# Fused soft-cap attention and soft mixture of experts: the tail products of a pair's first four tiles moved forward, constant products between the first transposes, and two more tiles of exponentials on VectorE

## The chip, the cores and the metric

The kernel runs on one core of one Trainium2 chip. The metric is the device time of one execution in microseconds (us), the median of several runs. Engines are called by the profiler's short names: PE is TensorE (PEld its weight loads), ACT is ScalarE, DVE is VectorE, POOL is GpSimd, SP is SyncE, which here only issues transfers.

## The reference

For each of 8 batches and 12 heads, with 448 tokens of 64 values, attention with a soft cap is computed; its output is the input x of a soft mixture of experts with 32 slots and 8 experts:

```
scores = cap * tanh(scale * q @ k.T / cap)          with cap = 30, scale = 1/8
attn = exp(scores - max), divided by its sum over the keys
x = attn @ v                                        3584 tokens of 768
logits = x @ phi                                    768 -> 32 slots
d = softmax of logits over all tokens;  c = softmax over the slots
slot_input = d.T @ x
slot_out[e] = relu(slot_input[e] @ w1[e]) @ w2[e]   4 slots for each expert e
out = c @ slot_out
```

(The lines say in short what the reference's Python computes.)

## The kernel before

**Tiles and pairs.** The 448 tokens of a head lie as 64 partitions with 7 tokens each. Two heads share the 128 partitions and are called a pair; there are 48 pairs, four heads (two pairs) make a quad Q, and three quads a batch. A pair has 7 key tiles c; one tile is 128 partitions (two heads of 64 keys) by 448 queries. All 336 tiles stand in one order (`turn`), in which the two pairs of a quad alternate, and are cut into 56 chunks j of 6 tiles. Seven chunks are one batch, the period in which the work repeats.

**A chunk.** PE computes the scores of three tiles at a time into one of two score buffers in PSUM (`qk_chunk`, L292). ACT takes the tanh of three tiles (`tanh_chunk`, L301) into a tile `ex` in SBUF; there are five such tiles (NEX), used in rotation, so that chunk j can only be written when the products that read chunk j-5 are done. ACT then takes the exponential of a whole chunk in place (`exp_chunk`, L305). In some chunks, the list `shared`, the first of the six tiles is left out of this and its exponential is computed by DVE in five steps, a polynomial (`poly_exp`, L327, L329 to L332): steps 0 and 1 in the slot a of the chunk's own iteration, 2 and 3 in its slot d, step 4 in the slot a of the next one. The exponential of a shared chunk covers 5 x 448 = 2,240 columns on ACT, of another 2,688.

**The product with v.** When all 7 tiles of a pair are there, PE multiplies them with v (`pv_mms`, L350). Queries are taken in three groups of 128 (128 x 128 weights) and a last group of 64, the tail, which takes two products of 64 x 64 a tile. A column of ones beside v gives the sum of the exponentials. The products of one pair gather in one PSUM bank (pool psV, one buffer). `pv_first` does the three large groups of tiles 0 to 3 (CA = 4), 12 products; `pv_rest` does those of tiles 4 to 6, 9 products, then the tails of tiles 0 to 3 (8 products) and of 4 to 6 (6 products), and ends with `norm`: DVE takes a reciprocal (L357) and multiplies the bank into xq (L358), which frees the bank for the next pair.

**The order of work.** It is written by hand. One iteration of the main loop emits the tanh of chunk j, the exponential of chunk j-1, then, if a pair is due, `pv_first`, slot a, the first scores for chunk j+1, slot b, `pv_rest`, slot c, the second scores, slot d. Everything else hangs in these slots: filling products on PE without use for the result (`fill`, L378, into unused columns of the pair's bank, and `spare` through `busy`, L589), the transposes of x (`x_transp`, L393 and L398, copied by DVE in L404), the transposes of the next quads' k and q (`transp`, L260, copied by DVE in L262), the cast of v on POOL (`vcast`, L270 and L271), logits, slot sums, and the loads of weights, which POOL issues. The transposes share one PSUM bank (pool psT). Each engine goes through its own instructions in the order in which they were emitted.

**The start.** Before the loop the first pair's q and k come in by small loads; 29 constant products run on PE (L589, `busy`), then `first_half(0)` casts, transposes and copies the first pair in pieces listed by hand (`first_pieces`, L215, L219, L221).

**After the loop** follow the last two pairs, the experts (from about 269 us) and the output.

Of the kernel before, what the change touches and what calls it, by code (L numbers as in the profile page):

```python
# [19 lines left out]
NT = 7  # L20
# [3 lines left out]
CS = 3  # L24
NG = 4
NF = 3
# [10 lines left out]
def kernel(  # L37
# [20 lines left out]
    cap = float(cap)  # L58
# [6 lines left out]
    NCH = NTILE // CH  # L65
# [3 lines left out]
    pe, dve, act, pool, sp = nc.tensor, nc.vector, nc.scalar, nc.gpsimd, nc.sync  # L69
# [109 lines left out]
    def load(nm, Q):  # L179
        if Q < NQ:  # L180
            t = raw_tile(nm)
            (sp if nm == "v" else pool).dma_start(out=t, in_=quad_ap(nm, Q))  # L182
            raws[nm, Q] = t
# [25 lines left out]
    def first_pieces(h, jobs):  # L209

        for stage, nm, c0, c1, eng, bank, at0 in jobs:
            copy = act.copy if eng is act else dve.tensor_copy
            cols = slice(h * HP, h * HP + HP)
            if stage == "cast":
                copy(casts[nm, 0][:, c0:c1, cols],  # L215
                     raws[nm, 0][h][:, c0 * DH:c1 * DH].rearrange("p (c d) -> p c d", d=DH))
            elif stage == "turn":
                for c in range(c0, c1):
                    pe.transpose(bank[cols, at0 + c - c0, :], casts[nm, 0][:, c, cols], ident)  # L219
            else:  # L220
                copy(qkT[nm, 0][cols, c0:c1, :], bank[cols, at0:at0 + c1 - c0, :])  # L221

    def first_half(h):
        for nm in ("k", "q"):
            if h == 0:
                qkT[nm, 0] = qk.tile([P, NT, P], BF16, name=nm + "T", tag=nm + "T")
        one = psT.tile([P, 8, P], BF16, name="ps1", tag="T")
        two = psV.tile([P, NT, P], BF16, name="ps2", tag="pv")
        if h == 0:

            first_pieces(h, (("cast", "k", 0, CS, dve, None, 0), ("cast", "q", 0, 4, dve, None, 0),
                             ("cast", "q", 4, NT, act, None, 0), ("turn", "k", 0, CS, pe, two, 0),
                             ("copy", "k", 0, CS, dve, two, 0), ("turn", "q", 0, 4, pe, one, 0),
                             ("cast", "k", CS, NT, act, None, 0),
                             ("copy", "q", 0, 4, dve, one, 0), ("turn", "q", 4, NT, pe, two, CS),
                             ("copy", "q", 4, NT, act, two, CS), ("turn", "k", CS, NT, pe, one, 4),
                             ("copy", "k", CS, NT, dve, one, 4)))
        else:
            first_pieces(h, (("cast", "k", 0, NT, dve, None, 0), ("cast", "q", 0, NT, dve, None, 0),
                             ("turn", "k", 0, NT, pe, two, 0), ("turn", "q", 0, NT, pe, one, 0),  # L240
                             ("copy", "k", 0, NT, dve, two, 0), ("copy", "q", 0, NT, dve, one, 0)))
            for nm in ("q", "k"):
                raws.pop((nm, 0)), casts.pop((nm, 0))
                load(nm, 2)
# [36 lines left out]
    scores, exs, pvs, xq, xTs, lgs = {}, {}, {}, {}, {}, {}  # L281
# [13 lines left out]
    def tanh_chunk(i):  # L295
        j, half = divmod(i, CH // CS)
        if half == 0:
            exs[j] = exps[j % NEX].tile([P, CH, S], BF16, name="ex", tag="ex")
        sc = scores.pop(i)
        for u0, u1 in ((0, 1), (1, CS)) if i == 0 else ((0, CS),):  # L300
            act.activation(exs[j][:, half * CS + u0:half * CS + u1, :],  # L301
                           sc[:, u0:u1, 0:S], ACT.Tanh, scale=qk_scale / cap)
# [4 lines left out]
    def exp_chunk(j):  # L307
        exp_part(j, 1 if j in shared else 0, CH)
# [3 lines left out]
    PARTS = {0: ((0, "a", (0, 1)), (0, "d", (2, 3)), (1, "a", (4,))),  # L312
             1: ((0, "a", (0, 1)), (0, "d", (2, 3)), (1, "a", (4,))),
             2: ((0, "a", (0, 1)), (0, "d", (2, 3)), (1, "a", (4,))),
             3: ((0, "a", (0, 1)), (0, "d", (2, 3)), (1, "a", (4,))),
             6: ((0, "a", (0, 1)), (0, "d", (2, 3)), (1, "a", (4,)))}
    shared = [j for j in range(NCH - 2) if j % 7 in PARTS and j > 7] if cap < 50 else []

    lead = POW2[0] / FRAC ** 3
    p2, p1, p0 = (c / POW2[0] * FRAC ** (n + 1) for n, c in enumerate(POW2[1:]))  # L320
# [15 lines left out]
    def pv_mms(pr, c0, c1, gs, dst):  # L336

        Q, h = divmod(pr, 2)
        for tail in (False, True):
            for c in range(c0, c1):  # L340
                j, u = divmod(place[pr, c], CH)
                for g in gs:
                    if (g == NF) != tail:
                        continue
                    for n in range(2 if tail else 1):
                        r = slice(n * HP, n * HP + HP) if tail else slice(0, P)
                        q0, s0 = g * P, 2 * (g - gs[0])
                        out_, v_ = (dst[r, s0, :], vbds[Q % 2][r, h, c, n * W:n * W + W]) \
                            if tail else (dst[:, s0:s0 + 2, :], vbds[Q % 2][:, h, c, :])
                        pe.matmul(out_, exs[j][r, u, q0:q0 + (HP if tail else P)], v_,  # L350
                                  start=(c == 0 and g == gs[0]), stop=(c == NT - 1),
                                  skip_group_check=True)

    def norm(pr, s0, s1, pv):
        Q, h = divmod(pr, 2)
        rec = xs.tile([P, NT, 1], F32, name="rec", tag="rec", bufs=4)[:, 0:s1 - s0, :]
        dve.reciprocal(rec, pv[:, 0:s1 - s0, DH:W])  # L357
        dve.tensor_tensor(xq[Q][:, h, s0:s1, :], pv[:, 0:s1 - s0, 0:DH],  # L358
                          rec.to_broadcast([P, s1 - s0, DH]), op=ALU.mult)
# [6 lines left out]
    CA, homes = 4, {}  # L366

    def pv_first(pr):
        xq_tile(pr)
        homes[pr] = psV.tile([P, 512], F32, name="pv", tag="pv")  # L370
        pvs[pr] = homes[pr][:, 0:NT * W].rearrange("p (t w) -> p t w", w=W)
        pv_mms(pr, 0, CA, (0, 1, 2), pvs[pr])

    def fill(n):

        home = homes[max(homes)][:, NT * W:]
        for _ in range(n):
            pe.matmul(home, ones, ones[:, 0:512 - NT * W], start=False, stop=True,  # L378
                      skip_group_check=True)

    def pv_rest(pr):
        pv_mms(pr, CA, NT, (0, 1, 2), pvs[pr])
        for c0, c1 in ((0, CA), (CA, NT)):
            pv_mms(pr, c0, c1, (NF,), pvs[pr][:, 2 * NF:NT, :])
        norm(pr, 0, NT, pvs.pop(pr))

    def turn_x(ps, q0, pr, gs):
# [12 lines left out]
    def x_transp(pr):  # L400
        ps = psT.tile([P, S], BF16, name="xps", tag="T")
        turn_x(ps, 0, pr, range(NG))
        t = xs.tile([P, S], BF16, name="xT", tag="xT", bufs=2)
        dve.tensor_copy(t, ps)  # L404
        xTs[pr] = t
# [38 lines left out]
    def e_norm(b):  # L444

        ps = psT.tile([P, 1], F32, name="zps", tag="T")
        for g in range(NG):
            r = slice(0, P if g < NF else HP)
            pe.matmul(ps, e4s[b][r, g, :], ones[r, 0:1], start=(g == 0), stop=(g == NG - 1))
        if b == 0:  # L450
            dve.tensor_copy(zacc, ps)
        else:
            dve.tensor_tensor(zacc, ps, zacc, op=ALU.add)
        if b == B - 1:
            dve.reciprocal(rz, zacc)
# [76 lines left out]
    for b in range(B):  # L532
        j = b * PER
# [44 lines left out]
    def run(j, slot):  # L578
        for f, a in aux.pop((j, slot), []):
            f(*a)  # L580
# [6 lines left out]
    def busy(n, home=None):  # L587
        for _ in range(n):
            pe.matmul(junk if home is None else home, ones, ones, start=True, stop=True)  # L589

    busy(4)
    junk = boots[1][:, 0, 0:P]
    busy(25)
    first_half(0)
    qk_chunk(0)
    qk_chunk(1)
# [6 lines left out]
    for j in range(NCH):  # L603
        run(j, "0")
        tanh_chunk(2 * j)
        if j == NCH - 1:
            exp_chunk(j - 1)
        tanh_chunk(2 * j + 1)
        run(j, "e")
        if j < 2:  # L610
            exp_chunk(j)
        elif 2 < j < NCH - 1:
            exp_chunk(j - 1)
        pr = pair_at.get(j - 2)
        if pr is not None:
            pv_first(pr)
        run(j, "a")
        if j == NCH - 1:
            pv_rest(pr)
            busy(8, psT.tile([P, P], F32, name="filler", tag="T"))  # L620
            e_norm(B - 2)
            x_transp(pr)

            id32 = xs.tile([P, P], F32, name="id32", tag="lg", bufs=2)
            pool.tensor_copy(id32, ident)
            break
        qk_chunk(2 * j + 2)
        run(j, "b")
        if pr is not None:
            pv_rest(pr)  # L630
        run(j, "c")
        qk_chunk(2 * j + 3)
        run(j, "d")
# [186 lines left out]
    for n in range(B // 2 * NT):  # L820
        bb, c = divmod(n, NT)
# [11 lines left out]
        for half in range(2):  # L833
            pe.matmul(op[:, half, 0:HD], et_tile(bb, c), so[half],
                      start=True, stop=True)
# [47 lines left out]
```

## Time and profile before

| | |
|---|---|
| median of 11 runs | 313.56 us (312.86 to 315.72) |
| profiled execution: its own time | 313.02 us |
| its span, from the first to the last instruction | 311.3 us |
| mean granted clock of TensorE | 0.984 |
| PE, ACT, DVE, POOL busy | 267.0, 272.7, 208.4, 134.0 us |
| HBM read, written | 91.32, 18.87 MB |

The profile is of one execution. Busy times are sums over the whole span and overlap between engines. Waits name the engine and line that ended an engine's idle time. The chain that ended last is followed back from the last instruction: at each step to what released it, or to the instruction before it on its engine. Starts of matrix products are recorded; their ends are modelled, so that a stretch of products is best measured from start to start.

### The profile page before, as it was taken

To read this page: it belongs to the slowest core of one execution; us is meant where nothing else is said; L and a number is where in the kernel's file an instruction comes from. 1 tells how busy PE (TensorE), PEld (TensorE's weight loads), DVE (VectorE), ACT (ScalarE), POOL (GpSimd) and SP (SyncE) were. 2 spreads that over 40 slices of the span, in tenths; PEclk is the share of its full clock that TensorE was granted. 3 is DMA by queue.
4 is the path that set the end of the run, shared out by engine and by line. 5 is a ranking of instruction groups with operands and counts; after the bars stand their busy time and mean duration, and the time that the engine had idled before them with its cause. 6 is when DMAs were issued, how large, how long until landed. Compare 5 with 4: busy or idle time off the path is not lost.

```text
span 311.3 us, 11337 instructions
## 1 busy us (share of the span) xinstructions
PE 267.0 (86%) x5063; PEld 189.4 (61%) x5063; DVE 208.4 (67%) x453; ACT 272.7 (88%) x209; POOL 134.0 (43%) x176
## 2 busy tenths in 40 slices
PE   8898888889998989998999899888999899998820
PEld 6675666666666666666666667666766678642400
DVE  3613358759975998499848995899478944236840
ACT  4999999999999999999999999999999997136730
POOL 4574373466447545653473448244912250000000
PEclk9999999999999999999999999999999999999985
DMA  7999999799999999999799999999999549938997
GB/s 238 234 203 202 204 177 192 146 225 200 207 187 219 211 194 188 221 196 212 132 201 202 211 189 205 205 201 204 193 203 202 143 133 324 336 150 314 392 412 298
DMA packets 57489, 67.75 MB, mean 218 GB/s; under 512 B 3809, under 2 KB 53601, under 8 KB 57441
## 3 DMA queue, kind: packets, MB, share of 16 engines
q0 software_dynamic: 42448, 35.31, 73.7%
q1 hardware_dynamic: 14704, 31.50, 29.8%
q8 instruction: 39, 0.64, 0.8%
q10 hardware_dynamic: 288, 0.23, 0.2%
q14 instruction: 10, 0.07, 0.1%
HBM read 91.32 MB, written 18.87 MB: 354 GB/s over the span
## 4 chain that ended last, share of the span: by engine, by line
PE 39%; DVE 38%; ACT 15%; issue 2%; DMA 1%; DVEq 0%; ACTq 0%
PE pv L350 10%; ACT ex L301 7%; DVE xq L358 6%; ACT ex L305 6%; DVE work L330 5%; DVE ex L332 4%; DVE work L331 4%; PE sc L292 4%; PE junk L589 4%; DVE work L329 3%; DVE xT L404 3%; DVE work L327 3%; PE kps L260 2%; DVE qT L262 2%; DVE kT L262 2%; PE so_ps L754 2%
## 5 line engine op out<-in xcount | busy, mean ns | idle before, releaser
L301 ACT ACTIVATE ex<-sc 128x1344 bf16<-128x1344 f32 (+1 forms) x113 | 143.6, 1376 | 3.5 <-PE pv L350 2.4
L305 ACT ACTIVATE ex<-ex 128x2240 bf16<-128x2240 bf16 (+4 forms) x58 | 130.8, 2259 | 0.1
L350 PE MATMUL pv<-vbd,ex 128*128 128x130 bf16 (+1 forms) x1610 | 86.4, 210 | 13.7 <-DVE xq L358 10.5
L350 PEld LDWEIGHTS <-ex 128*128 128x128 bf16 (+1 forms) x1680 | 72.4, 101 | 33.5 <-DVE xq L358 9.9
L292 PE MATMUL sc<-qT,kT 64*64 64x448 bf16 x672 | 69.6, 359 | 3.9 <-ACT ex L301 2.2
L270 POOL CAST vbd<-vraw 64x896 bf16<-64x896 f32 x23 | 21.4, 929 | 84.8 <-PE pv L350 81.0
L404 DVE COPY xT<-xps 128x448 bf16<-128x448 bf16 x47 | 18.3, 389 | 25.6 <-PE xps L398 24.9
L441 POOL COPY e<-E 128x512 bf16<-128x512 bf16 x9 | 5.5, 616 | 65.8 <-ACT E L435 31.7
L358 DVE TENSOR_TENSOR xq<-pv,rec 128x448 bf16<-128x448 f32 x46 | 28.7, 624 | 1.6
L330 DVE SCALAR_TENSOR_TENSOR work<-work 128x448 f32<-128x448 uint16 x33 | 26.9, 817 | 0.0
L292 PEld LDWEIGHTS <-kT 64*64 64x64 bf16 x672 | 21.7, 105 | 8.5 <-issue 5.6
L110 POOL DMA_DIRECT2D w1b<-in_moe_w_dram x32 | 24.7, 775 | 0.0
L589 PEld LDWEIGHTS <-ones 128*128 128x128 bf16 x320 | 19.5, 102 | 7.5 <-issue 4.3
L378 PE MATMUL pv<-ones 128*128 128x57 bf16 x620 | 23.9, 188 | 0.0
L271 POOL CAST vbd<-vraw 64x896 bf16<-64x896 f32 x23 | 22.4, 976 | 1.4
L589 PE MATMUL junk<-ones 128*128 128x128 bf16 x283 | 20.6, 220 | 1.7 <-DVE xq L358 1.3
L331 DVE SCALAR_TENSOR_TENSOR work<-work 128x448 f32<-128x448 f32 x33 | 21.3, 644 | 1.1
L262 DVE COPY kT<-kps 128x896 bf16<-128x896 bf16 x23 | 14.3, 622 | 11.4 <-PE kps L260 10.8
L332 DVE SCALAR_TENSOR_TENSOR ex<-work 128x448 bf16<-128x448 f32 x33 | 21.0, 636 | 0.2
L378 PEld LDWEIGHTS <-ones 128*128 128x128 bf16 x620 | 20.7, 96 | 0.3
L262 DVE COPY qT<-qps 128x896 bf16<-128x896 bf16 x23 | 14.3, 622 | 8.3 <-PE qps L260 8.3
L182 POOL DMA_DIRECT2D qb<-in_q_dram x22 | 16.4, 744 | 3.4 <-DVE casts L215 3.4
(117 smaller groups left out, 337.6 us busy)
## 6 DMA issues: line engine op xcount, KB each, us to landing
w1b<-in_moe_w_dram POOLq DMA_DIRECT2D x32, 384.0 KB, 8.7
vraw<-in_v_dram SPq DMA_DIRECT2D x23, 448.0 KB, 5.0
w2d<-in_moe_w_dram POOLq DMA_DIRECT2D x20, 384.0 KB, 9.2
w2t<-w2d SPq DMA_DIRECT2D x20, 384.0 KB, 5.1
out_dram<-ob SPq DMA_DIRECT2D x8, 768.0 KB, 7.1
qb<-in_q_dram POOLq DMA_DIRECT2D x22, 224.0 KB, 8.3
kb<-in_k_dram POOLq DMA_DIRECT2D x22, 224.0 KB, 7.1
w2b<-in_moe_w_dram POOLq DMA_DIRECT2D x12, 384.0 KB, 8.5
```

The source lines that it names most:

```text
L262: dve.tensor_copy(t, ps)
L292: pe.matmul(sc[cs, u, 0:S], qkT["k", Q][r, c, cs], qkT["q", Q][r, :, cs], start=True, stop=True)
L301: act.activation(exs[j][:, half * CS + u0:half * CS + u1, :], sc[:, u0:u1, 0:S], ACT.Tanh, scale=qk_scale / cap)
L305: act.activation(exs[j][:, u0:u1, :], exs[j][:, u0:u1, :], ACT.Exp, scale=cap)
L330: lambda: dve.scalar_tensor_tensor(xp, frac, p2, frac, ALU.add, ALU.mult),
L331: lambda: dve.scalar_tensor_tensor(xp, xp, p1, frac, ALU.add, ALU.mult),
L332: lambda: dve.scalar_tensor_tensor(t, xp, p0, xb, ALU.add, ALU.mult))
L350: pe.matmul(out_, exs[j][r, u, q0:q0 + (HP if tail else P)], v_, start=(c == 0 and g == gs[0]), stop=(c == NT - 1), skip_group_check=True)
L358: dve.tensor_tensor(xq[Q][:, h, s0:s1, :], pv[:, 0:s1 - s0, 0:DH], rec.to_broadcast([P, s1 - s0, DH]), op=ALU.mult)
L378: pe.matmul(home, ones, ones[:, 0:512 - NT * W], start=False, stop=True, skip_group_check=True)
L404: dve.tensor_copy(t, ps)
L589: pe.matmul(junk if home is None else home, ones, ones, start=True, stop=True)
```

## The change

Three edits are made together.

The 8 tail products of tiles 0 to 3 leave `pv_rest` and become a call of their own, `pv_tail(pr, 0, CA)`, after slot a of the pair's iteration and before the first scores for chunk j+1. For this, the flag `start`, which makes a bank begin anew, is given by the first large product of a pair alone and no longer by its first tail.

In the start's list, the word `fill` stands three times; each puts two constant products (`busy(2)`, 128 x 128 each) on PE: behind the transposes of the first four q tiles, behind those of the last q tiles, and behind those of the last k tiles.

In the list of shared chunks, j > 7 becomes j > 5, so that chunks 6 and 7 are shared too: 35 chunks in place of 33.

```diff
@@ first_pieces
-            if stage == "cast":
+            if stage == "fill":
+                busy(c0)
+            elif stage == "cast":
@@ first_half
-                             ("cast", "k", CS, NT, act, None, 0),
+                             ("cast", "k", CS, NT, act, None, 0), ("fill", "", 2, 0, pe, None, 0),
                              ("copy", "q", 0, 4, dve, one, 0), ("turn", "q", 4, NT, pe, two, CS),
-                             ("copy", "q", 4, NT, act, two, CS), ("turn", "k", CS, NT, pe, one, 4),
-                             ("copy", "k", CS, NT, dve, one, 4)))
+                             ("copy", "q", 4, NT, act, two, CS), ("fill", "", 2, 0, pe, None, 0),
+                             ("turn", "k", CS, NT, pe, one, 4), ("copy", "k", CS, NT, dve, one, 4),
+                             ("fill", "", 2, 0, pe, None, 0)))
@@ shared chunks
-    shared = [j for j in range(NCH - 2) if j % 7 in PARTS and j > 7] if cap < 50 else []
+    shared = [j for j in range(NCH - 2) if j % 7 in PARTS and j > 5] if cap < 50 else []
@@ pv_mms
-                                  start=(c == 0 and g == gs[0]), stop=(c == NT - 1),
+                                  start=(c == 0 and g == gs[0] < NF), stop=(c == NT - 1),
@@ pv_rest
+    def pv_tail(pr, c0, c1):
+        pv_mms(pr, c0, c1, (NF,), pvs[pr][:, 2 * NF:NT, :])
+
     def pv_rest(pr):
         pv_mms(pr, CA, NT, (0, 1, 2), pvs[pr])
-        for c0, c1 in ((0, CA), (CA, NT)):
-            pv_mms(pr, c0, c1, (NF,), pvs[pr][:, 2 * NF:NT, :])
+        pv_tail(pr, CA, NT)
         norm(pr, 0, NT, pvs.pop(pr))
@@ main loop
         if pr is not None:
             pv_first(pr)
         run(j, "a")
+        if pr is not None:
+            pv_tail(pr, 0, CA)
```

## The prediction

> **What bounds the kernel now.** I read the page first: PE 86%, ACT 88%, DVE 67% busy. Two engines at nearly the same share say that an average cannot name the bound, so I went on to the waits. From the page and then from the view of waits:
>
> ```profile
> PE 267.0 (86%) x5063; PEld 189.4 (61%) x5063; DVE 208.4 (67%) x453; ACT 272.7 (88%) x209; POOL 134.0 (43%) x176
> ...
> DVE rec L357 <- PE pv L350: 10.1, 20, 2.3
> ...
> ACT ex L301 <- PE pv L350: 2.4, 5, 0.8
> ...
> PE sc L292 <- ACT ex L301: 2.2, 3, 1.0
> ```
>
> ACT waits five times for PE to release a tile of exponentials (five buffers, NEX), and it does so only late. PE waits for ACT only three times, all before 49 us. The timeline of ACT tells when the late waits come:
>
> ```profile
> 142.67 2.22 ACT L305 ACTIVATE ex<-ex 128x2240 bf16<-128x2240 bf16 x1
> 145.32 2.47 ACT L301 ACTIVATE ex<-sc 128x1344 bf16<-128x1344 f32 x2 [0.43 <-PE pv L350]
> ```
>
> An exp of 2,240 columns holds ACT for 1.96 us where nothing waits (starts 49.17 and 51.13), so here 145.32 - 142.67 - 1.96 = 0.69 us are lost. Over the run such losses add up to about 4.3 us. Without them a period of seven chunks takes ACT 31.04 us (exp starts 57.97 and 89.01). But the start-to-start distance of the same xq product in the chain is 31.51, 31.68, 31.98, 31.93, 31.96 and 32.24 us (50.62, 82.13, 113.81, 145.79, 177.72, 209.68, 241.92): something slower than ACT sets it. The chain that ended last, from 141 to 179 us, has no ACT piece:
>
> ```profile
> 150.34 0.64 DVE xq L358
> ...
> 151.02 0.86 PE pv L350 x12
> ...
> 152.31 0.17 PE xps L398 x2
> ...
> 152.50 0.40 DVE xT L404
> 152.90 0.04 issue
> 152.95 0.58 PE kps L260 x14
> 153.53 0.89 PE pv L350 x19
> ...
> 157.11 0.40 DVE xT L404
> 157.51 0.04 issue
> 157.56 0.58 PE qps L260 x14
> 158.14 0.90 PE pv L350 x19
> ```
>
> So from 49 to 266 us the bound is PE and DVE in turns: ACT to about 48 us, then this relay, whose idle ACT only mirrors. The reader is to see the two places a period where PE's kps or qps waits for DVE's copy xT (they share the one psT bank). The timeline of PE shows what that wait costs:
>
> ```profile
> 148.07 0.56 PE L292 MATMUL sc<-qT,kT 64*64 64x448 bf16 x6
> 148.57 0.96 PE L350 MATMUL pv<-vbd,ex 128*128 128x130 bf16 x19
> ...
> 151.02 0.86 PE L350 MATMUL pv<-vbd,ex 128*128 128x130 bf16 x12 [0.63 <-DVE xq L358]
> 151.72 0.43 PE L378 MATMUL pv<-ones 128*128 128x57 bf16 x10
> ...
> 152.25 0.59 PE L292 MATMUL sc<-qT,kT 64*64 64x448 bf16 x6
> 152.95 0.58 PE L260 MATMUL kps<-ident,kb 128*64 128x128 bf16 x14
> ```
>
> Six score products hold PE 0.50 us when nothing follows late (148.07 to 148.57) and 0.70 us here: 0.20 us of idle PE.
>
> **Tails moved ahead of the first score chunk.** Eight products and their weight loads move; no DMA, copy or queue goes with them. Price of one: pv_first's twelve large products take 151.72 - 151.02 = 0.70 us, 0.058 each. In pv_rest, 9 large and 14 tails run from 153.46 to the next scores at 154.23, 0.77 us; less 9 x 0.058 that leaves 0.25 us, 0.0175 a tail. Eight cost 0.14 us. Where PE runs without a gap they are 0.14 us earlier in one place and 0.14 us less in another: the pair ends when it did. Where kps or qps waits for xT, the eight go into the 0.20 us gap and pv_rest ends 0.14 us sooner, on the chain. The chain shows this pattern at kps 57.83, 89.29, 120.98, 152.95, 184.88, 216.85 and qps 62.44, 93.90, 125.59, 157.56, 189.49, 221.46: 12 x 0.14 = 1.7 us. Bounds: nothing (the gap is not usable) to 12 x 0.20 = 2.4 us.
>
> What is queued behind the moved tails: the first score chunk, kps or qps, then pv_rest. The scores come 0.14 us later; ACT uses them 0.9 us or more after PE is done (scores from 143.20, tanh at 145.32), so nothing waits at first. DVE's copies of kT and qT start behind DVE's own queue (kT at 145.02, its transposes finished near 144.4), with slack of 0.5 us or more there. PE's tails wait for nothing new: pv_first needed the same four tiles just before.
>
> ACT's waits for buffers go. The tiles that tanh needs are read last by just these eight tails, now finished about 1.6 us sooner (143.4 in place of about 145.0); the longest wait was 0.77. I cost this at nothing, though it is 4.3 us of ACT: the relay does not wait for ACT after 49 us, and PE's scores come next as ACT's limit. If that cover is absent, it is the first rival. The changed start flag adds no instruction.
>
> **Two more tiles for VectorE.** Chunks 6 and 7 join, so two exps shrink from 2,688 to 2,240 columns: 2.33 to 1.96 us in ACT's steps (44.72 2.33 in the chain; 49.17 to 51.13), 0.37 each, 0.75 us, in the stretch where ACT is the bound. DVE gets ten instructions; mean rows 410 + 423 + 817 + 644 + 636 ns are 2.93 us a tile. From 36 to 40 us DVE is busy 0.62 of 4 us, so chunk 6 is covered. Chunk 7 is not wholly: its third step starts at about 41.7 beside the POOL casts of 41.06 and 42.04. Following DVE's order: third and fourth step to about 43.6, xT 44.0, last step 44.6, chunk 8's first two 45.35, reciprocal and xq to 46.2 in place of 46.02. PE's pair of 46.08 starts 0.2 late, but its scores waited 0.71 us for ACT at 48.28 and now wait no more: they start near 47.9. PE would gain 0.5; DVE, now without a break, reaches the reciprocal at about 50.2 for 50.38. I take 0.2 us gained. Bounds: 0.75 gained (all of ACT's) and 0.8 lost, one full collision of the kind in this answer on one line (ns, least, median, most):
>
> ```profile
> L330 DVE SCALAR_TENSOR_TENSOR work<-work x33: 614/616/1415, 46.2 to 247.2; 128x448 f32<-128x448 uint16 x33
> ```
>
> The Trainium skill, "SBUF — State Buffer", section "Who interferes with whom", speaks against this edit: a VectorE instruction with two SBUF inputs contends with a GpSimd one that reads SBUF, and the one that comes second waits for the whole of the other. The traced 616 against 1,415 ns agrees in kind. By the rule alone the third step would wait for the second cast's end at 42.99, and the 0.2 us would shrink to about nothing.
>
> **Six constant products at the start.** Two fit into the 0.22 us in which PE waits for DVE's kT copy (5.01), two before the k transposes of 5.48, which wait for ACT's cast; the last pair goes between transposes and scores (5.90), which wait for ACT's qT copy ending at 5.85. The granted clock is 1.00 in every slice from 4 to 8 us, so there is none to win back. A product costs 0.06 us (14 in 0.79, 160.76 to 161.55). I take nothing; bounds: 0.1 us gained, 0.36 lost (six, uncovered).
>
> **Sum.** 1.7 + 0.2 = 1.9 us on the profiled execution's 313.02 us (span 311.3, 1.7 around it): 311.1. That execution lies 0.54 under the median, so for the median 313.56 - 1.9 = 311.7 us. The likely case's own range: 310.3 (2.4, 0.75 and 0.1 gained) to 312.5 (half of the twelve gaps usable, 0.84, and 0.2).
>
> **Rivals.**
> ACT is the bound after all. For it: 88% and its late waits. Against: no ACT piece in the chain between 49 and 250 us. It would give back 4.3 + 0.75 us: 308.5. Chance 0.08.
>
> No measurable change (0.3%, 0.94 us, is about what a measurement can tell): the gap before kps is not usable, or DVE's queue, solid in most of a period, takes back what PE gains. For it: 145.02 to 154 DVE hardly pauses. Against: after both gated places DVE itself waits for PE (reciprocal at 154.55 and 159.14, 0.36 and 0.34 us idle), so there PE leads. It gives -0.2 to +0.3: 313.4. Chance 0.25.
>
> Slower: earlier ends of pv_rest start POOL's casts earlier against DVE, and one more two-input step a period collides in full. Price 1,415 - 616 = 0.80 us x 6 = 4.8, less 1.9: 316.5. It decides from 2.8 us on, 0.47 us a period. For it: the period already varies between 31.51 and 32.24 us with the length of L330 to L329 alone. Against: a shift of 0.14 us may as well part a pair that collides now (L330 at 146.91 took 1.06 beside a cast). Chance 0.11.
>
> The change doing nothing at all is excluded: the order of PE's instructions does change.
>
> **How the numbers follow.** 0.56 for the forecast, 0.08, 0.25 and 0.11 for the rivals. Faster by over 0.3% (under 312.6): nearly all of the first and the ACT case, 0.63. Same: 0.25 and a little of the first, 0.26. Slower: 0.11. The range leaves out the ACT case and the worse part of the slower one: 310.2 to 314.3.
>
> **What would show it.** ACT's wait for pv is gone or under 0.5 us in sum, and a wait of ACT for scores (sc L292) takes its place late; the exps count 35 of 2,240 and 20 of 2,688 columns; kps and qps still follow xT, but the scores before them hold PE 0.64 to 0.70 us with tails included in front; twelve reciprocals come 0.14 us sooner; the xq distances fall by about 0.28 us a period; the relay starts 0.2 us sooner near 50 us; the scores at the start stay at 5.90. The forecast is wrong if periods fall to 31.1 (ACT), stay (gap), or grow with L330 (collision).

## The result and the profile after

The changed kernel takes 310.53 us (median of 12 runs, 309.85 to 311.39); the kernel before, with the runs added since, 313.38 us (47 runs). By the medians it is about 2.9 us faster (0.9%), where 1.9 us were forecast. The ratio is 0.9901, with a 95% interval of 0.9885 to 0.9917, 3.1 us. The profiled execution took 310.19 us with a span of 308.4.

In the changed kernel the line numbers have moved: pv is L353, the scores are L295, the tanh is L304, kps and qps are L263, xT is L410, xq is L361, and the five polynomial steps are L330 and L332 to L335. The engines' busy time, share and instructions, from the page of the changed kernel:

```profile
PE 268.7 (87%) x5069; PEld 190.1 (62%) x5069; DVE 212.4 (69%) x463; ACT 271.5 (88%) x209; POOL 135.9 (44%) x176
```

Its view of waits (engine, line, what it waited for: us in all, times, longest):

```profile
DVE rec L360 <- PE pv L353: 8.0, 19, 2.3
...
PE sc L295 <- ACT ex L304: 1.3, 2, 0.8
ACT ex L304 <- PE sc L295: 1.2, 2, 1.0
```

ACT no longer waits for pv (2.4 us before). It waits for the scores, twice (once before, 0.8 us). The busy share of ACT has not moved although the kernel is faster. The timeline of PE in the changed kernel, at one of the places where kps waited for xT before (start, duration, instruction):

```profile
150.36 0.33 PE L399 MATMUL xps<-ident,xq 128*128 128x128 bf16 x3
150.62 0.22 PE L404 MATMUL xps<-ident,xq 64*64 64x64 bf16 x2
150.68 0.20 PE L353 MATMUL pv<-vbd,ex 64*64 64x65 bf16 x2
150.69 0.37 PE L295 MATMUL sc<-qT,kT 64*64 64x448 bf16 x1
...
150.80 0.54 PE L295 MATMUL sc<-qT,kT 64*64 64x448 bf16 x4
151.33 0.58 PE L263 MATMUL kps<-ident,kb 128*64 128x128 bf16 x14
151.84 0.83 PE L353 MATMUL pv<-vbd,ex 128*128 128x130 bf16 x11
152.48 0.38 PE L295 MATMUL sc<-qT,kT 64*64 64x448 bf16 x2
```

From the last small transposes to kps it is 151.33 - 150.62 = 0.71 us, and before it was 152.95 - 152.24 = 0.71: the eight tails stand in that time and cost nothing. From kps to the second scores it is 152.48 - 151.33 = 1.15 us; before it was 154.23 - 152.95 = 1.28. That is 0.13 us gained. The chain at this place (start, duration, piece):

```profile
150.97 0.38 PE sc L295 x4
151.35 0.56 PE kps L263 x14
151.91 0.77 PE pv L353 x11
...
155.83 0.56 PE qps L263 x14
156.39 0.85 PE pv L353 x15
```

Before, kps stood behind DVE's xT; now it stands behind PE's own scores. The gap is full.

The clearest measure is the time from one xq to the next. DVE makes one xq a pair, six a period, and all of them lie on the relay of PE and DVE. The steps are named by the iteration (j % 7) in which the later xq is made; values in us, from the starts of xq in the timeline of DVE:

| step into iteration | before | changed | tails moved in 4 and 5 only | tails moved elsewhere only | moved tails left out |
|---|---|---|---|---|---|
| 3 | 4.55 | 4.43 | 4.56 | 4.43 | 4.43 |
| 4 | 4.45 | 4.33 | 4.33 | 4.46 | 4.33 |
| 5 | 4.59 | 4.46 | 4.46 | 4.59 | 4.46 |
| 0 | 9.10 | 9.18 | 9.18 | 9.10 | 9.18 |
| 1 | 4.21 to 4.72 | 4.21 to 4.71 | 4.21 to 4.71 | 4.21 to 4.72 | 4.21 to 4.61 |
| 2 | 4.55 | 4.55 | 4.55 | 4.55 | 4.55 |

(The first and the last period differ in a few steps. In one period a step into 5 took 5.27 us with the tails moved in 4 and 5 only, which is told below. The last three columns are from the experiments below.)

### The profile page after: what moved, and what is told of

It is laid out like the page before. It is cut to its first block, busy times and chain, and to the rows that moved or that the text cites. A ratio compares the mean times of both kernels' runs of the same rounds, so it can differ in the third digit from the quotient of the medians.

```text
span 308.4 us, 11360 instructions
## 1 busy us (share of the span) xinstructions
PE 268.7 (87%) x5069; PEld 190.1 (62%) x5069; DVE 212.4 (69%) x463; ACT 271.5 (88%) x209; POOL 135.9 (44%) x176
## 4 chain that ended last, share of the span: by engine, by line
PE 43%; DVE 39%; ACT 12%; issue 2%; DVEq 0%; ACTq 0%
PE pv L353 11%; DVE xq L361 7%; ACT ex L304 6%; PE sc L295 5%; DVE work L333 5%; DVE work L334 5%; DVE ex L335 5%; ACT ex L308 5%; PE junk L595 4%; DVE work L332 4%; DVE work L330 3%; DVE kT L265 2%; DVE xT L410 2%; PE kps L263 2%; DVE qT L265 2%; PE pv L381 2%
## 5 line engine op out<-in xcount | busy, mean ns | idle before, releaser
L304 ACT ACTIVATE ex<-sc 128x1344 bf16<-128x1344 f32 (+1 forms) x113 | 158.5, 1629 | 1.3 <-PE sc L295 1.2
L308 ACT ACTIVATE ex<-ex 128x2240 bf16<-128x2240 bf16 (+4 forms) x58 | 143.8, 2484 | 0.1
L353 PE MATMUL pv<-vbd,ex 128*128 128x130 bf16 (+1 forms) x1610 | 94.3, 211 | 13.3 <-DVE xq L361 10.9
L353 PEld LDWEIGHTS <-ex 128*128 128x128 bf16 (+1 forms) x1680 | 75.9, 101 | 33.6 <-DVE xq L361 9.1
L295 PE MATMUL sc<-qT,kT 64*64 64x448 bf16 x672 | 72.4, 358 | 2.6 <-ACT ex L304 1.3
L273 POOL CAST vbd<-vraw 64x896 bf16<-64x896 f32 x23 | 21.4, 932 | 78.4 <-PE pv L353 74.4
L447 POOL COPY e<-E 128x512 bf16<-128x512 bf16 x9 | 6.3, 705 | 67.6 <-ACT E L441 33.6
L410 DVE COPY xT<-xps 128x448 bf16<-128x448 bf16 x47 | 18.3, 389 | 23.8 <-PE xps L404 23.0
L361 DVE TENSOR_TENSOR xq<-pv,rec 128x448 bf16<-128x448 f32 x46 | 28.7, 624 | 1.6
L295 PEld LDWEIGHTS <-kT 64*64 64x64 bf16 x672 | 24.9, 105 | 6.6 <-issue 4.3
L334 DVE SCALAR_TENSOR_TENSOR work<-work 128x448 f32<-128x448 f32 x35 | 24.4, 697 | 1.2
L274 POOL CAST vbd<-vraw 64x896 bf16<-64x896 f32 x23 | 23.4, 1019 | 1.4
L335 DVE SCALAR_TENSOR_TENSOR ex<-work 128x448 bf16<-128x448 f32 x35 | 21.6, 618 | 0.2
```

What stands on the lines that cost most here:

```text
L295: pe.matmul(sc[cs, u, 0:S], qkT["k", Q][r, c, cs], qkT["q", Q][r, :, cs], start=True, stop=True)
L308: act.activation(exs[j][:, u0:u1, :], exs[j][:, u0:u1, :], ACT.Exp, scale=cap)
L334: lambda: dve.scalar_tensor_tensor(xp, xp, p1, frac, ALU.add, ALU.mult),
L335: lambda: dve.scalar_tensor_tensor(t, xp, p0, xb, ALU.add, ALU.mult))
```

## The experiments

All ratios are against the kernel before, run on the same chip; its median there lay between 313.48 and 313.64 us.

### The parts alone

The tails alone: the diff of the main loop, `pv_rest` and the start flag, and nothing else.

> The tails' move alone, no constant products at the start, no new shared chunks. Theory gap (PE's idle 0.20 us before kps or qps, twice a period, now holds the eight tails): 12 x 0.13 us gained, with POOL's earlier casts up to 0.1 us a period more, so 1.6 to 2.3 us under the kernel before; the distance of the xq products near 31.6 in place of 31.95 us, the start of the relay near 50.6 us as before. Theory buffers (ACT's late waits were the bound): 4.3 us gained and a period near 31.1 us.

The two tiles alone: j > 7 becomes j > 5, and nothing else.

> Chunks 6 and 7 shared, nothing else. As predicted: 0.2 us gained, since DVE has no break near 50 us. Rival, from the changed kernel's profile, where the relay's xq came 0.19 us sooner although the start was 0.47 us later: 0.6 to 0.75 us gained, all that ACT saves; the xq of 50.62 us then comes near 49.95. The later periods stay as before (31.5 to 32.2 us), with ACT's waits for pv.

The constant products alone: the three entries `fill`, and nothing else.

> The six constant products at the start alone. Theory cost: they stand on the path of the first scores, 0.2 to 0.6 us slower, the first tanh near 7.1 us in place of 6.70. Theory clock phase (the first transposes of the changed kernel ran at half pace, 0.104 us apart, by chance of the run): about nothing in the median, and the first tanh between 6.7 and 6.9 us if the transposes run at 0.06 us.

The changed kernel without the constant products: the three entries `fill` taken out.

> The changed kernel without the constant products. Theory cost: 0.2 to 0.6 us faster than the changed kernel, 3.1 to 3.4 us under the kernel before. Theory clock phase: the same as the changed kernel, 2.85 us under the kernel before. The first tanh near 6.7 us if the transposes run at full pace; if they run at half pace without the products, the delay of the changed kernel was not theirs alone.

| kernel | median us | ratio (95%) |
|---|---|---|
| tails alone | 311.91 | 0.9930 (0.9903 to 0.9957) |
| two tiles alone | 313.18 | 0.9992 (0.9978 to 1.0006) |
| constant products alone | 313.28 | 0.9994 (0.9986 to 1.0003) |
| changed, without constant products | 310.58 | 0.9907 (0.9895 to 0.9920) |

The tails carry most of the gain, about 2.2 us by the ratio and 1.7 by the medians. The constant products change nothing that can be measured, alone or on top of the rest. The tiles alone are inside the noise, but their profile shows a gain at 50 us. Since the starts of the executions differ, it is counted from the first xq: to the xq near 50 us it is 26.64 us (23.88 to 50.52), and 27.17 both in the kernel before (23.45 to 50.62) and with the constant products alone (24.03 to 51.20). So 0.5 us are won of the 0.75 that ACT saves, and part is lost again: at the xq near 242 us 0.3 are left (218.22 us from the first xq, against 218.56 with the constant products alone and 218.47 before).

In the profile of the tails alone PE stands still once, in the middle of moved tails, and the view names nothing that it waits for:

```profile
125.44 0.22 PE L352 MATMUL pv<-vbd,ex 64*64 64x65 bf16 x2 [0.62 <-issue]
```

The step into 5 is 5.22 us there in place of 4.46, 0.76 us lost. The same is seen at the same place with the tails moved in 4 and 5 only (0.68 us) and in the last version below (0.42), and in none of the other ten profiles. What it is stays open, and so does how often it falls into the runs that were not profiled.

What the tiles gave PE: the following lines are from the timelines of PE, first of the tiles alone:

```profile
47.66 0.33 PE L399 MATMUL xps<-ident,xq 128*128 128x128 bf16 x3
47.92 0.22 PE L404 MATMUL xps<-ident,xq 64*64 64x64 bf16 x2
47.98 0.57 PE L294 MATMUL sc<-qT,kT 64*64 64x448 bf16 x6
```

and of the constant products alone, at the same work:

```profile
48.86 0.38 PE L295 MATMUL sc<-qT,kT 64*64 64x448 bf16 x4 [0.72 <-ACT ex L304]
```

The scores follow the small transposes after 0.06 us, not after the 0.22 us that the record gives as their duration. The pair's products start at the same time in both (46.65 and 46.66 us), and PE wins 0.88 us here. The reciprocal that follows then waits for PE no more: it starts at 50.28 behind DVE's own copy of kT, against 50.96 behind PE's products with the constant products alone.

### Is ACT's wait the cause or the mirror?

The kernel before with a sixth buffer of exponentials; to make room, four blocks of w2 less are kept in SBUF:

```diff
-NEX = 5
+NEX = 6
-    for nm in ("ex1", "ex2", "vb0", "ex3", "ex4", "ex0", "vb1"):
+    for nm in ("ex1", "ex2", "vb0", "ex3", "ex4", "ex0", "vb1", "ex5"):
-    R2 = 24
+    R2 = 20
```

> The kernel before with a sixth buffer of exponentials (NEX = 6), so that ACT need not wait for the tails of the pair four chunks back; to make room four blocks of the second weights less are kept in SBUF (R2 = 20), which adds one store and two loads of 384 KB at the end's side. Nothing of the tails is moved. Theory gap: ACT's waits for pv vanish and the xq distances stay at 31.5 to 32.2 us; the time stays within 1 us of the kernel before. Theory buffers: the distances fall towards 31.1 and 2 to 4 us are gained.

The time is 316.82 us, ratio 1.0087 (1.0062 to 1.0112). The expected limit of 1 us did not hold (3.3 us slower), but the loss is not in the relay. The waits of ACT in this kernel:

```profile
ACT ex L301 <- PE sc L292: 1.9, 4, 0.8
```

Its wait for pv has gone, and the relay goes on as before: from the xq at 50.99 us to that at 242.49 are 191.50 us, and 191.30 before (50.62 to 241.92); the forecast of the other theory, periods near 31.1 us, did not come. The loss is at the end, where the stored blocks come late. From the chain that ended last:

```profile
278.82 0.49 ACT so L804
...
279.35 7.78 DMA w2t<-w2d
287.14 0.04 issue
287.18 0.37 PE so_ps L754 x4
```

So ACT's late waits did not bound the kernel: taken away, they give nothing back to the relay.

### Which of the moved tails matter

One kernel moves the tails only where kps or qps waits for xT and PE sets the next step, the other moves only the rest. The edit, on the kernel with tails alone (in the second, `not in`):

```diff
+        if pr not in early:
+            pv_tail(pr, 0, CA)
         pv_tail(pr, CA, NT)
...
-        if pr is not None:
+        if pr is not None and j % 7 in (4, 5):
+            early.add(pr)
             pv_tail(pr, 0, CA)
```

> The kernel before with the eight tails moved ahead only in the two iterations a period (j % 7 = 4 and 5) where kps or qps waits for DVE's xT and PE sets the next step; elsewhere they stay. Theory gap: 12 x 0.13 = 1.5 us gained of the 1.7 to 2.2 that all moved tails give. Theory buffers: the late waits of ACT came at the iteration j % 7 = 2, which is left as before, so ACT still waits and little is gained.

> The other half: the tails move ahead in all iterations but j % 7 = 4 and 5. Theory gap: 0 to 0.7 us gained, by POOL's earlier casts alone, although ACT's waits for pv of 0.4 to 0.8 us vanish. Theory buffers: most of the gain, 1.5 us or more.

In iterations 4 and 5 only: 312.65 us, ratio 0.9962 (0.9947 to 0.9976). Elsewhere only: 312.67 us, 0.9969 (0.9954 to 0.9984). By the ratios about 1.2 and 1.0 us (0.9 each by the medians); together as much as all moved tails. The table of steps shows each share. Moved in 4 and 5, the steps into 4 and 5 fall by 0.12 and 0.13 us, as forecast, and the step into 0 grows by 0.08, so that a period wins 0.17 and not 0.25. Moved elsewhere, only the step into 3 falls, by 0.12, and the 1 us lies between the two forecasts. The prediction had priced that step at nothing. It goes with the tails of iteration 2: this step runs through DVE's own queue from xq to xq, POOL's two casts now start sooner against it, and DVE's third polynomial step ends sooner. The lines, from the timelines of DVE and POOL, before:

```profile
145.79 0.62 DVE L358 TENSOR_TENSOR xq<-pv,rec 128x448 bf16<-128x448 f32 x1
146.54 0.95 POOL L271 CAST vbd<-vraw 64x896 bf16<-64x896 f32 x1
146.91 1.06 DVE L330 SCALAR_TENSOR_TENSOR work<-work 128x448 f32<-128x448 uint16 x1
148.00 0.62 DVE L331 SCALAR_TENSOR_TENSOR work<-work 128x448 f32<-128x448 f32 x1
```

and with the tails moved elsewhere only:

```profile
145.49 0.62 DVE L360 TENSOR_TENSOR xq<-pv,rec 128x448 bf16<-128x448 f32 x1
146.12 0.95 POOL L273 CAST vbd<-vraw 64x896 bf16<-64x896 f32 x1
146.57 0.98 DVE L332 SCALAR_TENSOR_TENSOR work<-work 128x448 f32<-128x448 uint16 x1
147.59 0.63 DVE L333 SCALAR_TENSOR_TENSOR work<-work 128x448 f32<-128x448 f32 x1
```

The second cast starts 0.75 us after xq before and 0.63 after the edit; the fourth step follows xq by 2.21 and 2.10 us. It moves with the cast. This pair of lines speaks for the collision; below, in the experiment on the step that varies, the same two casts come later by accident, and this step grows.

ACT still waits for pv in both halves: 2.4 us in all, four times, with the tails moved in 4 and 5 only (before: 2.4, five times); 2.0 us, three times, with them moved elsewhere only. Each half alone leaves the wait nearly whole, and each gains about 1 us: the wait is no measure of the gain. What was expected of ACT's waits in the second half did not come.

### What is left of the moved tails' price

The kernel without constant products, and the eight tails left out of the main loop:

```diff
-        if pr is not None:
-            pv_tail(pr, 0, CA)
```

> The changed kernel without the constant products, and with the eight tails of tiles 0 to 3 left out of the main loop altogether (for 46 pairs the last 64 queries then see only tiles 4 to 6). 46 x 0.14 = 6.4 us less work for PE. Theory gap: at the three places a period where the step to the next xq fell by 0.13 us the moved tails are already free, so only the two pairs between 243 and 253 us that PE runs through without a break gain, 0.3 to 0.6 us in all against the same kernel with its tails. Rival: the moved tails still stand on the path, and 2 us or more are gained.

Every step of a period but the varying one is the same to 0.01 us as with the tails in their new place (last column of the table); the three last pairs, which PE runs through without a break, fall by 0.12 to 0.14 us each (4.61 to 4.49, 4.09 to 3.96, 3.99 to 3.85). From the first to the last xq it is 231.68 us, and 232.75 with the tails. So the moved tails are free but for about 1 us, more than the 0.3 to 0.6 that I had expected: 0.39 at the end, 0.35 in the varying step and 0.28 in one early step (8.95 to 8.67). The median, 311.20 us (0.9938, 0.9915 to 0.9962), is not lower than with the tails (310.58). In the profiled execution (313.46 us, the slowest of six) that is the start: its first xq comes at 26.53 us, against 23.90. What its start looks like is told below; for the other runs of this kernel it is not known.

### The step that varies, and a further version

POOL's casts for every third quad one iteration later, on the changed kernel without constant products:

```diff
         quad_in(3 * b + 3, (j + 4, "a"), (j + 5, "a"), (j + 4, "b"), (j + 5, "b"),
-                (j + 7, "d"))
+                (j + 8, "d"))
```

> The changed kernel without the constant products, and POOL's two casts of v for the third quad of a batch emitted one iteration later (from the slot d of j + 7 to that of j + 8). Theory collision (the one xq step a period that varies, 4.21 to 4.72 us, is lengthened by POOL's casts and transfer issues against DVE's polynomial): that step comes down to 4.2 to 4.3 in all periods, up to 1.5 us gained, unless the casts collide as much one iteration later. Rival (the step varies with the slot's own work): the step stays between 4.2 and 4.7.

313.31 us, ratio 1.0001 (0.9971 to 1.0030): 2.7 us slower than with the casts in their place. The varying step did come down, to between 4.21 and 4.28 us in five periods (4.37 in the first, 4.32 in the last). But the casts hardly moved: in these five periods they start 0.26 to 0.31 us before the xq that opens the step, and 0.28 to 0.47 us before it without the edit. What moved are POOL's issues of the next k and q, which lay behind the casts and now lie ahead of them. Without the edit, from the timelines of DVE and POOL:

```profile
138.61 0.73 POOL L182 DMA_DIRECT2D qb<-in_q_dram  x1
138.91 0.65 DVE L331 TENSOR_SCALAR work<-work 128x448 uint16<-128x448 uint16 x1
```

and with it:

```profile
141.02 0.39 DVE L331 TENSOR_SCALAR work<-work 128x448 uint16<-128x448 uint16 x1
```

This second polynomial step takes 0.65, 0.68 and 0.73 us in three of the five periods without the edit and 0.39 or 0.40 in all five with it: 0.3 of the 0.5 us by which the step varies. In the other two it takes 0.39 beside such an issue too, so what decides is not shown. The remainder goes with which of the two is lengthened, DVE's third step or POOL's second cast. So the step is set by what POOL does beside it, the issues above all, and not by the casts alone.

The loss is in the step into 3, which rose from 4.43 to between 4.68 and 5.36 in six periods. The casts beside it are those of the next quad. Their load is issued after the moved casts; it lands late (7.5 us after 139.36), and they wait for it. From the view of waits:

```profile
POOL vbd L272 <- DMA vraw<-in_v_dram: 31.6, 5, 7.0
```

and around one of the five places, from the timelines of DVE and POOL:

```profile
147.06 0.93 POOL L272 CAST vbd<-vraw 64x896 bf16<-64x896 f32 x1 [7.03 <-DMA vraw<-in_v_dram]
147.19 1.28 DVE L332 SCALAR_TENSOR_TENSOR work<-work 128x448 f32<-128x448 uint16 x1
148.05 1.23 POOL L273 CAST vbd<-vraw 64x896 bf16<-64x896 f32 x1
148.50 1.25 DVE L333 SCALAR_TENSOR_TENSOR work<-work 128x448 f32<-128x448 f32 x1
```

The first cast starts 0.95 us after the xq of 146.11 here; without the edit it starts 0.36 us before it (143.89, 144.25), and the two DVE steps take 0.99 and 0.63 us. Together they are 0.9 us longer, as much as the step into 3 (5.36 for 4.43). This is the collision that the pair of lines above spoke for.

Chunks 3, 4 and 5 shared too, in the stretch that ACT sets (two more entries of `PARTS`, for 4 and 5):

```diff
-    shared = [j for j in range(NCH - 2) if j % 7 in PARTS and j > 5] if cap < 50 else []
+    shared = [j for j in range(NCH - 2) if 2 < j < 8 or (j > 7 and j % 7 not in (4, 5))] if cap < 50 else []
```

> The changed kernel without the constant products and with chunks 3, 4 and 5 shared too (38 shared chunks). ACT sets the pace to about 48 us and saves 0.37 us a chunk, 1.1 us in all; DVE is busy less than half of that stretch. Theory slack: 0.5 to 1.1 us faster than without these three, 3.4 to 4.0 us under the kernel before. Rival: PE, 91% busy from 20 to 36 us, becomes the pace there and 0 to 0.4 us are gained.

310.15 us, ratio 0.9877 (0.9856 to 0.9899): the lowest median of all, but its interval overlaps that of the changed kernel. The expected 0.5 us are there at 50 us (25.98 us from the first xq, against 26.49) and gone near 257 (232.78 against 232.75): the varying step took 4.43, 4.43 and 4.71 us in three periods in place of 4.21, 4.34 and 4.45.

Both together:

> Chunks 3, 4 and 5 shared as before, with the later casts. If the collision theory holds, the 0.6 us that the three chunks gained by 50 us and lost again in the varying step are kept: 0.5 us or more faster than with the casts at their old place, about 309.5 us. If not, 310.0 to 310.5 us.

314.67 us, ratio 1.0022 (0.9994 to 1.0050). The expected 309.5 us did not come; the later casts spoil this one too.

## Why the prediction was right or wrong

**The bound.** Right. From about 50 us the relay of PE and DVE sets the time, and ACT's waits for buffers only mirror it. The sixth buffer shows it: no wait for pv, and the relay as long as before (191.50 and 191.30 us).

**Tails, 12 x 0.14 = 1.7 us.** The mechanism was right and the size nearly so: 0.12 to 0.13 us at each of the twelve places. The scores before kps hold PE 0.64 us with the tails in front, as forecast; but kps and qps do not follow xT any more, as was also forecast, they follow these scores. Two terms were missing. The first: the step into 0 gives back 0.08 us a period. It is seen in PE's transposes eps and DVE's copy of them, ET, from the timelines before:

```profile
159.40 0.47 PE L462 MATMUL eps<-ident,e 128*128 128x128 bf16 x4
159.92 0.39 DVE L463 COPY ET<-eps 128x448 bf16<-128x448 bf16 x1
```

and of the changed kernel:

```profile
157.61 0.47 PE L468 MATMUL eps<-ident,e 128*128 128x128 bf16 x4
158.12 0.39 DVE L469 COPY ET<-eps 128x448 bf16<-128x448 bf16 x1
```

ET starts 0.54 us after the xq of 159.38 before and 0.62 after that of 157.50 now, and in both 0.51 to 0.52 us after eps. From the start of qps, xq comes 0.13 us sooner than before (1.82 and 1.69 us), but PE's second scores start after 1.30 us in both, and eps behind them come only 0.04 us sooner (1.84 and 1.80). So ET, and PE's lps behind it, start later against xq. No run isolates this; it is read from these starts. The second: the step into 3 gains 0.12 us a period. The prediction named the shift of POOL's casts only under the slower rival, as a loss; that it might as well be a gain stood there as an argument against, without a price. In sum the tails alone gave 2.2 us by the ratio (0.9930, 0.9903 to 0.9957) and 1.7 by the medians. From the first to the last xq it is 1.2 us in their profile (234.51 against 235.71 before), and 2.0 without the one stall of 0.76.

**Nothing for ACT's freed buffers.** Right: the waits for pv are gone, and by the sixth buffer they were worth nothing.

**Two more tiles, 0.2 us.** Too small: 0.53 us from the first xq to that near 50 us, in the upper half of the range up to 0.75. That the xq of chunk 8's iteration would be 0.2 us late was nearly right: the step to it is 4.29 us with the tiles and 4.15 or 4.16 without. The term that was mis-sized is "DVE, now without a break, reaches the reciprocal at about 50.2 for 50.38". From the xq before it to this reciprocal the tiles' profile has 4.31 us (45.97 to 50.28), the kernel before 4.98 (45.40 to 50.38), and the forecast had about 4.6. I had added whole durations. Successive instructions overlap: in the profile before, a last step of 0.62 us starts at 148.85 and the next one at 149.38, 0.53 later. In the tiles' profile the nine durations from xq to the reciprocal add up to 4.54 us, and they took 4.31 with a wait of 0.20 for PE among them. The rule of the Trainium skill, "SBUF — State Buffer", section "Who interferes with whom", was weighed for this place; what ran there is this, from the timelines of DVE and POOL of the tiles alone:

```profile
42.22 0.68 DVE L332 SCALAR_TENSOR_TENSOR work<-work 128x448 f32<-128x448 uint16 x1
42.48 1.24 POOL L273 CAST vbd<-vraw 64x896 bf16<-64x896 f32 x1
42.94 1.26 DVE L333 SCALAR_TENSOR_TENSOR work<-work 128x448 f32<-128x448 f32 x1
```

The third step came first and the cast was lengthened (1.24 for 0.95), then the fourth step (1.26 for 0.62). That agrees with the rule in kind: the one that came second was lengthened each time. But the sentence of the prediction on this rule had the order the other way round, with the third step waiting. About 0.6 us of DVE were lost, most of it on slack; 0.13 is the lateness of that xq.

**Constant products, nothing.** Right (0.9994, 0.9986 to 1.0003), but the forecast that the first scores stay at 5.90 us was wrong: they started at 6.37 in the profile of the changed kernel. The products are not the cause: without them they started at 6.35, and the first tanh at 7.14 for 7.17. The last section tells more.

**The start of the relay, 0.2 us sooner near 50 us.** That the two profiles show this (50.43 for 50.62) is luck: the first xq came 0.48 us later (23.93 for 23.45), and from there on 0.67 us were gained, 0.53 by the tiles and 0.12 by the tails, each as in its own profile (26.64 and 27.05 us for 27.17).

**The sum.** 1.9 us forecast, about 2.9 measured. From the first to the last xq it is 235.71 us before and 232.70 in the changed kernel, 3.0 us less: 2.0 by the tails (without the stall), where 1.7 were forecast, and 0.5 by the tiles, where 0.2 were. The other 0.4 come only with both: 0.17 in the first step into 3 (4.44 us, against 4.61 with the tails alone and 4.59 with the tiles alone) and 0.26 in one varying step near 137 us (4.46, against 4.72 in both). Why these two fall only together is not shown. Of the rivals, "ACT is the bound" falls with the sixth buffer, and "the gap is not usable" with the steps. The slower one, collisions of POOL with DVE, is a real price in this kernel (up to 0.9 us in one step where the casts come late), but this change moved it the other way.

## What to carry to other kernels

Where two engines have the same busy share, take away the waits of one and see whether the rhythm changes; here a sixth buffer took away ACT's, and the relay stayed as it was. Work is free where it goes into a place that the next instruction waits out anyway: find these places by comparing the same group's start-to-start time where it is followed at once and where it is not. When a chain is added up by hand, add start-to-start times, not durations, and see where a moved step lands against an engine that shares something with its neighbour, because a shift of 0.1 us can gain or lose several times as much.

## What the runs showed of the hardware that was not expected

The pace of PE at the start is not the same in every execution. The transposes of the first pair (up to 6.5 us), from the profile before and then from that of the changed kernel without constant products (ns: least, median, most, then first and last start):

```profile
L219 PE MATMUL ps<-ident,casts x14: 216/219/243, 4.2 to 5.7; 128*64 128x128 bf16 x14
```

```profile
L221 PE MATMUL ps<-ident,casts x14: 216/300/314, 4.4 to 6.0; 128*64 128x128 bf16 x14
```

In ten of the thirteen profiles the first tanh comes between 6.91 and 7.28 us, with the constant products and without them. In two, the kernel before and the one with the tails moved elsewhere only, it comes at 6.70 and 6.77, and in the one with the tails left out at 7.67. The granted clock reads 1.00 in all of them from 0 to 8 us, also over the first 29 products, which came about 0.107 us apart, while the same products come 0.056 us apart later. So this column does not show it, and the pace is read from start to start. In the profile with the tails left out the slow pace lasted longest. Its transposes of the second pair:

```profile
L221 PE MATMUL ps<-ident,casts x14: 264/311/311, 9.6 to 10.9; 128*64 128x128 bf16 x14
```

These 14 transposes took 1.65 us from 9.56 us (0.94 in the profile before, from 7.72). Constant products were 0.107 us apart up to 13.8 us and 0.056 from there on, the granted clock read 1.00 there too, and the relay began 2.6 us late. Whether the constant products make such long starts rarer was not tried.
